# Order of the first loads and of one transpose step in a fused sliding-window attention and MLP kernel

## The chip, the cores and the metric

The kernel runs on one core of one Trainium2 chip. The metric is device time in microseconds: 308.39 us before the change, the median of three runs (308.27 to 308.43).

## The reference, cut to what matters

```python
# q, k, v: (8 batches, 8 heads, 576 positions, 64), f32
scores = scale * q @ k.T                    # scale = 1/8
mask = abs(pos[:, None] - pos[None, :]) <= 32
attn = softmax(where(mask, scores, -1e9))
x = (attn @ v).transpose(0, 2, 1, 3).reshape(4608, 512)
h = x @ w_in                                # (512, 2048)
g = where(h >= 1, h, where(h <= -1, 0, (h + 1) ** 2 / 4))
out = g @ w_out                             # (2048, 512), f32
```

## The kernel before

The inputs are f32 and everything is multiplied in bf16. All loads but two are issued by GpSimd, which casts them on the way. Two heads lie side by side in the 128 partitions, and the positions are cut into 9 chunks of 64; `vn` therefore has 18 chunks of v for one batch, chunks 0 to 8 for one pair of head groups (`y1 = 0`) and 9 to 17 for the other (`y1 = 1`).

```python
# S = 576, D = 64, NY = 4, NC = 9, DFF = 2048, NF = 8, TB = 256
def load_half(half, t, h, ...):      # half of q (t=0) or k (t=1) of batch 0, for 64 columns
    (eng or nc.gpsimd).dma_start(out=dst[0, half][:, h], in_=...)       # line 86

def load_rows(b, t):                 # q or k of batch 1, whole
    nc.gpsimd.dma_start(out=dst[b], in_=...)                            # line 93

def load_v(b, n):                    # a quarter of v of batch b: 64 partitions
    ...
    nc.gpsimd.dma_start(out=vn[b][64 * a:64 * a + 64, :, h], in_=...)   # line 107

def load_w_in(c0, c1, h):            # columns c0 to c1 of w_in, 64 partitions
    nc.gpsimd.dma_start(out=w_in[64 * h:64 * h + 64, :, c0:c1], in_=...)  # line 111

def load_w_out(c, k0, k1):           # 256 columns of w_out, rows of blocks k0 to k1
    nc.gpsimd.dma_start(out=w_out[:, k0:k1, 256 * c:256 * c + 256], in_=...)  # line 116
```

The loads at the start, in the order in which they are issued:

```python
for h in range(2):
    load_half(0, 0, h, (nc.sync, nc.scalar)[h], q32)    # q, first half: not GpSimd
for h in range(2):
    load_half(0, 1, h)                                  # k, first half
...
load_v(0, 0)
P.affine_select(out=step, ...)
for n in range(1, 4):
    load_v(0, n)
...
cuts = [0, 256, 512, 768, 1024, 1280, 1792, DFF]
w = [(load_w_in, c0, c1, h) for c0, c1 in zip(cuts, cuts[1:]) for h in range(2)]
put(w[:4] + [(load_half, 1, t, h) for t in range(2) for h in range(2)] + w[4:12])
put([(load_w_out, 0, 0, 4)] + w[12:])
put([(load_w_out, 0, k, k + 4) for k in range(4, 16, 4)] + [(load_rows, 1, t) for t in range(2)])
put([(load_v, 1, n) for n in range(4)])
```

The main loop goes through 144 positions, called slots here. In slot `a` the first product makes 256 columns of h for 256 tokens (`f = a % 8`, so slot `a` of the first eight reads w_in's columns 256a to 256a + 255), ScalarE and VectorE make g of it, and other work is hung behind the slot:

```python
def project(hp, f, r0, todo, first, last):              # hp has two buffers
    for n, (j, kk) in enumerate(todo):
        nc.tensor.matmul(hp[:, j], w_in[:, kk, 256 * f + 128 * j:...], xT[:, kk, r0:r0 + TB], ...)  # line 489

for a in range(...):
    post = [...]                     # output steps: pairs = [(6, 0), (7, 1), (8, 2), (9, 3), (11, 4), (12, 5), ...]
    ...
    project(...)                     # slots 0 and 1 together, then one by one
    A.activation(rr, hp, AF.Relu, scale=0.5, bias=0.5)  # line 533
    if a in (1, 7, 8, 9, 10, 11, 12):
        A.activation(mx, rr, AF.Square)                 # line 536
        V.scalar_tensor_tensor(g, hp, 1.0, mx, op0=ALU.max, op1=ALU.min)   # line 537
    else:
        V.tensor_max(mx, hp, rr)                        # line 539
        V.scalar_tensor_tensor(g, rr, 1.0, mx, op0=ALU.min, op1=ALU.mult)  # line 540
    run(a)                           # attention work that stands at this slot
    for x in post:
        pair(x)                      # the output step: 8 matmuls of g with four blocks of w_out, line 464
```

Before slot 0 the kernel makes the first 256 tokens of batch 0's attention: transposes of q's and k's first halves, scores, `sums(0, 0, 0, TB)` and `sums(0, 1, 0, TB)`, each of which multiplies with `vn` and with ones (line 295) and ends in ScalarE's ln and exp (lines 301, 302) and VectorE's product into xT (line 307). What stands at the slots that matter here:

```python
at(1, (tposes, 0, (0, 1), (1, 1)))                  # second halves of q and k of batch 0
at(2, (scores, 0, (0, 1), (0, 2), (2, 4)), (scores8, 0, ps_o))
at(3, (scores, 0, (1, 2), (0, 2), (2, 4), ps_n), (sums, 0, 0, TB, MAIN, ps_s))
at(4, (sums, 0, 1, TB, MAIN))                       # y1 = 1, tokens 256 to 479
at(5, (sums, 0, 0, MAIN, S, ps_s))                  # tokens 480 to 575
at(13, seq[0][1])                                   # first scores of batch 1
...
for t in range(2):
    at(11 + t, (tposes, 1, (t, 0), (t, 1)))         # q of batch 1 behind slot 11, k behind slot 12
```

`tposes` is 36 transposes on TensorE (line 189) and four copies out of PSUM (line 192), two on ScalarE and two on VectorE.

Of the kernel before, what the change touches and what calls it, by code (L numbers as in the profile page):

```python
# [14 lines left out]
def kernel(  # L15
# [19 lines left out]
    nc = tc.nc  # L35
    B, H, S, D = q.shape
    NT, DM, DFF = out.shape[0], 512, 2048
    NY = H // 2
    NC = S // 64
# [38 lines left out]
    qn, kn, vn = {}, {}, {}  # L78
# [20 lines left out]
            nc.gpsimd.dma_start(out=x[:, :, h], in_=src[b, NY * h:NY * h + NY].rearrange("y s d -> (y s) d")  # L99
                                .rearrange("(u p) d -> p u d", p=128))  # L100

    def load_v(b, n):
        if b not in vn:
            vn[b] = nat.tile([128, 2 * NC, 2, D], BF, name="vn", tag="vn", bufs=3)
        h, a = divmod(n, 2)
        y = NY * h + 2 * a
        nc.gpsimd.dma_start(out=vn[b][64 * a:64 * a + 64, :, h], in_=v[b, y:y + 2].rearrange("y s d -> (y s) d")  # L107
                            .rearrange("(c r) d -> r c d", r=64))

    def load_w_in(c0, c1, h):  # L110
        nc.gpsimd.dma_start(out=w_in[64 * h:64 * h + 64, :, c0:c1],  # L111
# [11 lines left out]
    for h in range(2):  # L123
# [5 lines left out]

    step = early.tile([128, 257], BF, name="step")  # L130
    V.memset(step, 0.0)
    load_v(0, 0)
    P.affine_select(out=step, in_=step, compare_op=ALU.is_ge, fill=-1.0, base=-65, channel_multiplier=-1,
                    pattern=[[1, 257]])
    for n in range(1, 4):
        load_v(0, n)
    V.memset(ones, 1.0)
    for t in qTs:
        V.memset(t[:, 0:PAD], 0.0)
# [4 lines left out]
    def put(todo):  # L144
        for fn, *x in todo:
            fn(*x)

    cuts = [0, 256, 512, 768, 1024, 1280, 1792, DFF]
    w = [(load_w_in, c0, c1, h) for c0, c1 in zip(cuts, cuts[1:]) for h in range(2)]
    put(w[:4] + [(load_half, 1, t, h) for t in range(2) for h in range(2)] + w[4:12])  # L150
    put([(load_w_out, 0, 0, 4)] + w[12:])
    put([(load_w_out, 0, k, k + 4) for k in range(4, 16, 4)] + [(load_rows, 1, t) for t in range(2)])
    put([(load_v, 1, n) for n in range(4)])
    P.tensor_copy(band[HD[1], 0:128], band[HD[1], 64:192])
    for m, n, x in ((mask4, 8, 128), (mask8, 4, TAIL)):
# [229 lines left out]
    def at(a, *todo):  # L385


        ev.setdefault(a, []).extend(x for x in todo if x)
# [24 lines left out]
    for n, a in enumerate(sl):  # L413
        at(a, seq[6 + n][0], seq[7 + n][1] if n < len(sl) - 1 else None)
    for t in range(2):
        at(11 + t, (tposes, 1, (t, 0), (t, 1)))
    loads, xps = {}, {16: [(2, 0)], 18: [(2, 1)]}
    for b in range(LONG + 1, B):
        a = sl[5 * (b - 1) - 7] - 17
# [75 lines left out]
    for a in range(NF * NB + 2 * NF):  # L495
# [11 lines left out]
        if a < NF * NB:  # L507
            if wide:
                n, f = divmod(a - WIDE[0], 2 * NF)
                t = WIDE[0] // NF + 2 * n  # L510
# [6 lines left out]
            else:  # L517
                t, f = divmod(a, NF)
# [30 lines left out]
        if a >= 40:  # L549
            n = (4, 3, 3)[a % 3] if a < 88 else 4  # L550
# [36 lines left out]
```

The softmax here doesn't subtract the row's maximum and nothing guards it: scores larger than these inputs give would overflow.

## Time and profile before

| what | value |
| --- | --- |
| time, median of three | 308.39 us |
| span of the profiled run | 306.1 us |
| granted TensorE clock | 1.00 |
| TensorE matmuls, share of the span | 97% |
| VectorE, ScalarE, GpSimd | 78%, 62%, 25% |
| start of the first slot | 13.24 us |
| idle time of TensorE before that slot and slots 1, 2 and 11 | 0.44, 0.67, 0.72, 0.33 us |

The page of a profile gives busy times and the chain of work that ended last. A timeline lists the instructions of an engine in order of time, with equal neighbours merged: start, length, engine, line, operation, the tiles that it writes and reads, the shape and a count; in brackets stand the idle time just before it and what ended it. PE is TensorE, PEld its weight loads, DVE is VectorE, ACT is ScalarE, POOL is GpSimd, SP is SyncE. A bar of GpSimd that issues a load is not the transfer; the landing of a load is told apart, as the time from the bar's start. The view by stretches gives each engine's busy time within a stretch, with the number of instructions, then the granted clock, the share of the DMA engines and GB/s, counted in the bytes that are written.

### The profile page before, as it was taken

How to read it: one execution, taken by the hardware profiler on the slowest of the kernel's cores; microseconds unless marked ns; L12 is line 12 of the kernel's file. 1: busy time of each engine (PE TensorE's matmuls, PEld its weight loads, DVE VectorE, ACT ScalarE, POOL GpSimd, SP SyncE). 2: the span in 40 equal slices, each digit the busy share in tenths (PEclk: the TensorE clock that was granted, in tenths of full speed). 3: DMA queues.
4: the chain of work that ended last, by engine and by line, in shares of the span. 5: the costliest groups of instructions: out<-in, count | busy, mean ns of one | idle time of the engine just before them, and what ended most of it. 6: DMA issues, size and time to landing. Idle time of an engine off the chain costs nothing.

```text
span 306.1 us, 7974 instructions
## 1 busy us (share of the span) xinstructions
PE 298.4 (97%) x3388; PEld 181.2 (59%) x3388; DVE 239.6 (78%) x376; ACT 191.2 (62%) x320; POOL 77.1 (25%) x92
## 2 busy tenths in 40 slices
PE   8889999999999999999999999999999999999995
PEld 3468878876666676666654544444445444446644
DVE  3268568888888989998999998888888888788700
ACT  3688896748856856776766766665667654444311
POOL 8787661037009009004600900000000000000000
PEclk9999999999999999999999999999999999999999
DMA  9999999999999999999998991550101000000121
GB/s 153 184 197 198 186 196 153 173 156 164 139 186 109 181 169 124 165 144 116 148 127 166 145 156 39 111 115 34 36 34 37 36 34 35 36 34 34 59 80 69
DMA packets 137171, 35.67 MB, mean 117 GB/s; under 512 B 122160, under 2 KB 132912, under 8 KB 137136
## 3 DMA queue, kind: packets, MB, share of 16 engines
q0 software_dynamic: 102976, 18.06, 83.5%
q1 hardware_dynamic: 34016, 16.81, 26.1%
q8 instruction: 26, 0.43, 0.6%
q10 hardware_dynamic: 144, 0.29, 0.3%
q14 instruction: 9, 0.07, 0.1%
HBM read 36.70 MB, written 9.44 MB: 151 GB/s over the span
## 4 chain that ended last, share of the span: by engine, by line
PE 91%; POOL 3%; DMA 2%; ACT 1%; issue 1%; DVE 0%; POOLq 0%; ACTq 0%
PE op L449 36%; PE hp L489 22%; PE hp L514 18%; PE bb L295 6%; PE op L464 4%; PE bb L229 2%; DMA w_in<-in_moe_w_in_dram 2%; POOL vn L107 1%; PE op L440 1%; POOL w_in L111 1%; PE tp L189 1%; ACT pt L237 1%; POOL kh L86 1%; POOL qh L86 0%; PE bb L208 0%
## 5 line engine op out<-in xcount | busy, mean ns | idle before, releaser
L533 ACT ACTIVATE rr<-hp 128x512 f32<-128x512 f32 x144 | 85.5, 595 | 86.1 <-PE hp L514 41.7
L449 PE MATMUL op<-w_out,gT 128*128 128x512 bf16 x496 | 126.9, 380 | 0.0
L539 DVE TENSOR_TENSOR mx<-hp,rr 128x512 f32<-128x512 f32 x137 | 94.4, 689 | 26.1 <-ACT rr L533 24.3
L540 DVE SCALAR_TENSOR_TENSOR gT<-rr,mx 128x512 bf16<-128x512 f32 x137 | 94.8, 692 | 4.7
L489 PE MATMUL hp<-xT,w_in 128*128 128x256 bf16 x640 | 83.1, 273 | 2.2 <-DMA w_in<-in_moe_w_in_dram 1.4
L489 PEld LDWEIGHTS <-w_in 128*128 128x128 bf16 x640 | 61.8, 98 | 22.7 <-issue 2.8
L449 PEld LDWEIGHTS <-gT 128*128 128x128 bf16 x496 | 46.1, 98 | 45.2
L514 PE MATMUL hp<-xT,w_in 128*128 128x512 bf16 x256 | 65.7, 379 | 0.0
L514 PEld LDWEIGHTS <-w_in 128*128 128x128 bf16 x256 | 25.0, 98 | 30.2
L99 POOL DMA_DIRECT2D qn<-in_q_dram x12 | 14.6, 1224 | 89.5 <-DMA kT<-kn 87.4
L237 ACT ACTIVATE pt<-bb 128x1024 bf16<-128x1024 f32 (+1 forms) x33 | 32.7, 1001 | 4.5 <-PE bb L229 3.1
L107 POOL DMA_DIRECT2D vn<-in_v_dram x32 | 27.7, 900 | 4.8 <-DMA w_out<-in_moe_w_out_dram 4.0
L307 DVE TENSOR_TENSOR xT<-bb,rc 128x512 bf16<-128x512 f32 (+1 forms) x32 | 21.0, 657 | 9.6 <-ACT rc L302 8.7
L453 ACT COPY osb<-op 128x512 f32<-128x512 f32 x31 | 18.0, 580 | 11.4 <-PE op L449 11.1
L302 ACT ACTIVATE rc<-lr 128x512 f32<-128x512 f32 (+2 forms) x40 | 23.5, 587 | 1.3
L301 ACT ACTIVATE lr<-bb 128x512 f32<-128x512 f32 (+2 forms) x40 | 22.1, 552 | 0.3 <-PE bb L295 0.3
L203 DVE TENSOR_TENSOR pt<-pt,mask 128x1024 bf16<-128x1024 bf16 (+1 forms) x33 | 20.3, 614 | 0.5 <-ACT pt L237 0.5
L295 PE MATMUL bb<-pt,ones 64*64 64x256 bf16 (+3 forms) x352 | 19.6, 255 | 0.1
L295 PE MATMUL bb<-pt,vn 64*64 64x128 bf16 (+3 forms) x712 | 18.4, 204 | 0.1
L295 PEld LDWEIGHTS <-ones 64*64 64x64 bf16 x352 | 10.3, 105 | 11.6 <-issue 11.6
L295 PEld LDWEIGHTS <-vn 64*64 64x64 bf16 x712 | 16.7, 107 | 0.3 <-DMA vn<-in_v_dram 0.3
L464 PE MATMUL op<-w_out,gT 128*128 128x256 bf16 x128 | 16.5, 273 | 0.0
(61 smaller groups left out, 140.3 us busy)
## 6 DMA issues: line engine op xcount, KB each, us to landing
out_dram<-osb SPq DMA_DIRECT2D x35, 256.0 KB, 2.3
vn<-in_v_dram POOLq DMA_DIRECT2D x32, 144.0 KB, 9.7
qn<-in_q_dram POOLq DMA_DIRECT2D x12, 288.0 KB, 6.2
kn<-in_k_dram POOLq DMA_DIRECT2D x12, 288.0 KB, 9.0
w_in<-in_moe_w_in_dram POOLq DMA_DIRECT2D x12, 128.0 KB, 5.6
w_out<-in_moe_w_out_dram POOLq DMA_DIRECT2D x4, 256.0 KB, 8.0
w_out<-in_moe_w_out_dram POOLq DMA_DIRECT2D x2, 512.0 KB, 13.2
kh<-in_k_dram POOLq DMA_DIRECT2D x4, 144.0 KB, 5.4
```

Source lines behind the costliest of these rows:

```text
L107: nc.gpsimd.dma_start(out=vn[b][64 * a:64 * a + 64, :, h], in_=v[b, y:y + 2].rearrange("y s d -> (y s) d") .rearrange("(c r) d -> r c d", ...
L237: A.activation(p, ps[:, :, :w * n].rearrange(like, y=m), AF.Exp, scale=D ** -0.5)
L295: nc.tensor.matmul(bb[HD[h], a, o + c0:o + c1], ones[HD[a]] if c is None else vn[b][HD[a], c, h], p(a, h), start=n == 0, stop=True, skip_g ...
L301: A.activation(lr[:, :, :D0], bb[:, :, D0:2 * D0], AF.Ln)
L302: A.activation(rc[:, :, :D0], lr[:, :, :D0], AF.Exp, scale=-1.0)
L449: nc.tensor.matmul(op[tt], gT[:, j, home(tt // 2), 128 * (tt % 2):128 * (tt % 2) + 128], w_out[:, j], start=j == 0, stop=j == 15)
L464: nc.tensor.matmul(o[:, tt], gT[:, j, p, 128 * tt:128 * tt + 128], w_out[:, j, 256 * half:256 * half + 256], start=not done, stop=len(done ...
L489: nc.tensor.matmul(hp[:, j], w_in[:, kk, 256 * f + 128 * j:256 * f + 128 * j + 128], xT[:, kk, r0:r0 + TB], start=first and n == 0, stop=l ...
L514: nc.tensor.matmul(hp.rearrange("p n t -> p (n t)"), w_in[:, kk, 128 * f:128 * f + 128], xT[:, kk, r0:r0 + 2 * TB], start=n == 0, stop=n == 3)
L533: A.activation(rr, hp, AF.Relu, scale=0.5, bias=0.5)
L539: V.tensor_max(mx, hp, rr)
L540: V.scalar_tensor_tensor(g, rr, 1.0, mx, op0=ALU.min, op1=ALU.mult)
```

## The change

Three things are changed, and no arithmetic.

1. The first v (batch 0) is loaded in two parts: chunks 0 to 13 where it stood, and chunks 14 to 17 later. The first part is all that the sums before slot 0 and those behind slot 3 read; chunks 14 to 17 are first read behind slot 4. The four loads of the second part are put one by one behind the four loads of w_in for slots 2 and 3.
2. w_in is loaded in pieces of 256 columns throughout. Before, the columns of slots 5 and 6 (1280 to 1791) came in one piece of 512, so that slot 5 waited for slot 6's columns too. The first load of w_out still stands in front of the last two pieces.
3. The transposes of q of batch 1 stand behind slot 10 instead of slot 11. Those of k stay behind slot 12.

The aim is to let slots 0 to 3 start with fewer bytes ahead of them in the queue, to let slot 5 start on its own columns, and to put work on TensorE between slots 10 and 11.

```diff
-    def load_v(b, n):
+    def load_v(b, n, c0=0, c1=2 * NC):
...
-        nc.gpsimd.dma_start(out=vn[b][64 * a:64 * a + 64, :, h], in_=v[b, y:y + 2].rearrange("y s d -> (y s) d")
-                            .rearrange("(c r) d -> r c d", r=64))
+        nc.gpsimd.dma_start(out=vn[b][64 * a:64 * a + 64, c0:c1, h], in_=v[b, y:y + 2].rearrange("y s d -> (y s) d")
+                            .rearrange("(c r) d -> r c d", r=64)[:, c0:c1])
...
-    load_v(0, 0)
+    load_v(0, 0, 0, 14)
...
     for n in range(1, 4):
-        load_v(0, n)
+        load_v(0, n, 0, 14)
...
-    cuts = [0, 256, 512, 768, 1024, 1280, 1792, DFF]
-    w = [(load_w_in, c0, c1, h) for c0, c1 in zip(cuts, cuts[1:]) for h in range(2)]
-    put(w[:4] + [(load_half, 1, t, h) for t in range(2) for h in range(2)] + w[4:12])
-    put([(load_w_out, 0, 0, 4)] + w[12:])
+    w = [(load_w_in, c, c + 256, h) for c in range(0, DFF, 256) for h in range(2)]
+    put(w[:4] + [(load_half, 1, t, h) for t in range(2) for h in range(2)]
+        + [x for n in range(4) for x in (w[4 + n], (load_v, 0, n, 14, 2 * NC))] + w[8:14])
+    put([(load_w_out, 0, 0, 4)] + w[14:])
...
     for t in range(2):
-        at(11 + t, (tposes, 1, (t, 0), (t, 1)))
+        at(10 + 2 * t, (tposes, 1, (t, 0), (t, 1)))
```

## The prediction

> **What bounds the kernel now.** I read the page's busy line first, then the chain that ended last, then the timelines of TensorE and GpSimd over the first 42 us, then the landing times of single loads.
>
> ```profile
> PE 298.4 (97%) x3388; PEld 181.2 (59%) x3388; DVE 239.6 (78%) x376; ACT 191.2 (62%) x320; POOL 77.1 (25%) x92
> ...
> PE 91%; POOL 3%; DMA 2%; ACT 1%; issue 1%; DVE 0%; POOLq 0%; ACTq 0%
> ```
>
> TensorE is the bound: 97% busy and 91% of the chain. What is not TensorE in the chain (POOL 3%, DMA 2%) lies at the start: printed in order of time, the chain is GpSimd issuing loads up to 12 us, then 6.31 us of a w_in load, and from 18.53 us TensorE nearly without a break. The change moves only what comes before slot 13, so I work with the timeline of that stretch. TensorE (start, length, what, and in brackets the idle time before it and what ended it):
>
> ```profile
> 13.24 0.60 PE L489 MATMUL hp<-xT,w_in 128*128 128x256 bf16 x4 [0.44 <-DVE xT L307]
> 14.50 1.47 PE L489 MATMUL hp<-xT,w_in 128*128 128x256 bf16 x12 [0.67 <-DMA w_in<-in_moe_w_in_dram]
> ...
> 17.12 0.69 PE L189 MATMUL tp<-ident,kh 128*64 128x128 bf16 x17 [0.47 <-DMA kh<-in_k_dram]
> 18.53 1.03 PE L489 MATMUL hp<-xT,w_in 128*128 128x256 bf16 x8 [0.72 <-DMA w_in<-in_moe_w_in_dram]
> ...
> 26.99 1.04 PE L489 MATMUL hp<-xT,w_in 128*128 128x256 bf16 x8
> 27.86 1.04 PE L464 MATMUL op<-w_out,gT 128*128 128x256 bf16 x8
> ...
> 32.23 1.04 PE L489 MATMUL hp<-xT,w_in 128*128 128x256 bf16 x8
> 33.59 1.03 PE L489 MATMUL hp<-xT,w_in 128*128 128x256 bf16 x8 [0.33 <-DVE gT L537]
> 34.55 1.20 PE L189 MATMUL tp<-ident,qn 128*64 128x128 bf16 x36
> 35.68 1.05 PE L464 MATMUL op<-w_out,gT 128*128 128x256 bf16 x8
> ```
>
> Slots 0 and 1 start at 13.24, slot 2 at 18.53, slot 7 at 26.99, slot 10 at 32.23, slot 11 at 33.59. The reader is to see five pauses: 0.44 for xT, then 0.67, 0.47 and 0.72 for loads, then 0.33 in front of slot 11 for VectorE's gT of slot 9 (hp has two buffers). GpSimd, which issues every load with a cast:
>
> ```profile
> 11.42 1.95 POOL L111 DMA_DIRECT2D w_in<-in_moe_w_in_dram  x3
> 14.65 1.83 POOL L111 DMA_DIRECT2D w_in<-in_moe_w_in_dram  x3 [1.28 <-DMA w_in<-in_moe_w_in_dram]
> 16.65 1.33 POOL L111 DMA_DIRECT2D w_in<-in_moe_w_in_dram  x2 [0.17 <-issue]
> ```
>
> Of these loads the one at 14.65 is the eighteenth. It starts 0.28 after the tenth landed (issued 8.38, 6.0 to landing, so 14.37). The twenty-first starts at 16.65, 0.28 after the thirteenth landed (16.36). So I read a rule into it: **a load waits until the load eight before it has landed.** Last, the DMA rate, from the view by stretches (busy time of the engines, then PEclk, DMA share, GB/s):
>
> ```profile
> 6.00:10.00 4.00, 3.81 (x85) 2.45 (x83) 1.35 (x2) 2.57 (x5) 3.99 (x7) 1.00 2.72 152
> 10.00:14.00 4.00, 3.29 (x67) 1.74 (x65) 0.91 (x2) 3.39 (x6) 3.07 (x6) 1.00 1.38 199
> 14.00:18.00 4.00, 2.84 (x48) 2.24 (x48) 2.24 (x4) 2.40 (x5) 3.05 (x5) 1.00 1.35 195
> ```
>
> The rate is flat at 195 to 199 while w_in is loaded, and 152 while v is loaded. The queue does not run dry: the loads are served in order, and each waits for the bytes ahead of it.
>
> **What the Trainium skill says.** "DMA: Bandwidth & Descriptors", section "Why small descriptors are slow (HBM only)", has a fixed cost on every descriptor, 27% for one of 256 bytes; v is read in rows of 64 f32, that is 256 bytes, and the trace agrees (152 against 195 GB/s). "Perfetto Trace Analysis", section "DMA Optimizations", says that splitting a load helps it start sooner if the DMA engines are otherwise idle; here they are not, so I expect the splits to change the order of arrival and not the total. The same page, section "DMA Instruction — SWDGE (GPSIMD)", says that the bar on GpSimd is descriptor generation and not the transfer; the trace agrees: a w_in bar is 0.61, its landing 4.6 to 6.4 after its start.
>
> **The change part by part.**
>
> *Part 1, the first v cut to 14 chunks.* Four loads lose 4 of 18 chunks: 4 x 64 partitions x 4 chunks x 128 bytes written = 131 kB. At 152 GB/s that is 0.86 us by which everything behind the v loads arrives earlier: w_in of slots 0 and 1, then q's and k's second halves. What this opens on TensorE: the v wait inside the first sums (0.31 on the weight loads) goes, so xT comes some 0.25 earlier, since ScalarE is busy with pt until 10.93 and its ln now starts at 11.20. The 0.67 pause goes (the load lands at about 13 instead of 14.37); k's half lands at 16.2 instead of 17.08; slot 2's w_in, with one v piece (0.2) ahead of its second half, lands at 17.7 instead of 18.40. Slot 2 should start at 17.6 to 17.9, a lead of 0.6 to 0.9.
>
> *Part 2, the v pieces and the split w_in.* The same 131 kB come back between w_in's pieces, so from slot 4's w_in on no bytes are saved. New are 6 loads: 4 v pieces and 2 halves of w_in. Each costs GpSimd about 0.6 (a w_in bar has 256 descriptors, as a v piece has), 3.6 in all; the shortened v bars give back little (an estimate: 0.89 for 1152 descriptors and 0.61 for 256 make 0.3 ns each, so 4 x 256 x 0.3 = 0.3 us). GpSimd waits 1.28 + 0.42 + 0.50 + 0.73 between loads today, so most of the 3.6 fits there, but with eight loads in flight and four of them only a third as long, fewer bytes are queued. An estimate with the bars, the landing spread and the eight-load rule put in order by hand: the queue runs dry for 1.0 to 1.5 us in total between the third v piece and slot 4's w_in. The slowest of the DMA engines should hide about 1.2 of that, because I take it to be behind the others today: the w_in load at 8.38 landed 1.9 after the one before it (14.37 against 7.78 + 4.7), where 0.67 is usual, and the delay stays. What remains, with two 512-column loads cut (2.6 between landings for both today, against 4 x 0.67), is +0.1 to +0.4 for everything behind slot 5's w_in. Slot 5's own w_in comes about 1.2 earlier (22.6 instead of 23.70), since it no longer waits for slot 6's half.
>
> *What becomes of the lead.* The second output step at 27.86 needs the second piece of w_out, issued at 20.08 and landing 7.7 later, at 27.80: **no slack today.** All the bytes ahead of it are the same after the change. So the lead of 0.6 to 0.9 at slot 2 ends there: the step starts at 27.9 to 28.2, that is 0 to 0.3 later than today. The early gain is swallowed.
>
> *Part 3, q's transposes in slot 10.* TensorE's work is only reordered: slot 11's 8 matmuls (0.98 in the chain) and 36 transposes (1.12) change places. Today the 0.33 pause plus start-up before slot 11 is lost: slot 10 ends at about 33.2, slot 11 starts at 33.59. After, the transposes need q of batch 1, issued at 22.74 and landing 10.6 later, 33.34; with +0.1 to +0.4 it lands at 33.45 to 33.75. They start there, end 1.12 later, slot 11 follows (0.98), and the next output step starts at 35.55 to 35.85, against 35.68 today.
>
> *Sum.* -0.13 to +0.17 at 35.7 us, from these steps alone. Behind it TensorE runs on; k's transposes at 37.53 need a load that lands at 36.18 (1.3 of slack), v of batch 1 lands at 41.16 for sums at 42.76 (1.6 of slack). The later stages have no changed instruction, so the shift is carried to the end.
>
> **Rivals.** *A: the lead survives.* If the DMA queue has slack that I do not see, because v pieces are served beside w_in at less cost, w_out and q land earlier, and up to 0.9 us of the lead at slot 2 plus the 0.33 pause would reach the end: 307.2 to 307.6. For it: the rate of 152 for v means that the DMA engines are not at their byte limit there. Against it: the flat 195 to 199 after. *B: GpSimd becomes the bound.* If the eight-load rule starves the queue by more than the slowest engine's lag, w_out and q land 0.6 to 1.0 later, and slot 10's transposes stall TensorE where slot 11 used to run: 308.8 to 309.3. For it: 6 more loads and a wait of 1.28 that exists already. Against it: 2.9 us of waits between loads that can absorb them. *C: nothing is moved*, because the q load decides either way: 308.2 to 308.4. This is nearest to my sum.
>
> **Range and chances.** I lean a little to the fast side of the sum, as A costs nothing to be partly true and the 0.33 pause is sure to go: 308.1, with 307.4 (most of A) to 308.8 (mild B) for 8 in 10. A move of 2% would be 6.2 us; all pauses of this stretch together are 0.44 + 0.67 + 0.47 + 0.72 + 0.33 = 2.6 us, so neither side of 2% can be reached this way.
>
> **What would show it.** Slot 2's first matmul at 17.6 to 17.9 shows part 1 right. A pause in front of the second output step at about 28, ended by w_out, shows the lead swallowed; no pause and a start under 27.5 shows rival A. The transposes of q behind slot 10 with a wait of 0.1 to 0.5 for the q load, and no gT wait before slot 11, show part 3. GpSimd pauses before the third and fourth v piece and before slot 4's w_in, with a DMA rate under 190 GB/s from 17 to 20 us, show the starved queue. The prediction is wrong if q of batch 1 lands before 33.0 or after 34.0, or if a stage after 50 us changes its waits by more than a few tenths.

## The result and the profile after

The changed kernel takes 310.66 us (median of six runs, 310.31 to 311.26), against 308.35 us (308.11 to 308.57) for six runs of the kernel before on the same chip: a ratio of 1.0075, with a 95% interval of 1.0062 to 1.0088. It is slower by 2.3 us, and outside the range. The profiled span is 308.5 us against 306.1.

From the page of the kernel after, the line of busy times and the shares of the chain that ended last:

```profile
PE 293.6 (95%) x3350; PEld 181.4 (59%) x3388; DVE 240.0 (78%) x376; ACT 191.6 (62%) x320; POOL 80.4 (26%) x98
...
PE 85%; DMA 7%; POOL 4%; issue 2%; ACT 1%; POOLq 0%; ACTq 0%
```

The chain has changed: DMA holds 7% of it instead of 2%. Its longest pieces in order of time (start, length, what) name the loads:

```profile
8.49 5.62 DMA qh<-in_q_dram
16.90 2.41 POOL w_in L111 x4
19.32 5.94 DMA w_in<-in_moe_w_in_dram
25.54 10.49 DMA qn<-in_q_dram
36.07 1.20 PE tp L189 x36
```

Up to 36 us the end is now set by a wait of GpSimd for q's half, by GpSimd's issuing, and by the loads of w_in and of q of batch 1. TensorE's timeline shows the same from its side:

```profile
13.13 1.03 PE L489 MATMUL hp<-xT,w_in 128*128 128x256 bf16 x8
...
17.62 1.05 PE L489 MATMUL hp<-xT,w_in 128*128 128x256 bf16 x8 [0.92 <-DMA w_in<-in_moe_w_in_dram]
...
22.42 1.03 PE L489 MATMUL hp<-xT,w_in 128*128 128x256 bf16 x8 [0.89 <-DMA w_in<-in_moe_w_in_dram]
...
26.07 1.03 PE L489 MATMUL hp<-xT,w_in 128*128 128x256 bf16 x8 [0.69 <-DMA w_in<-in_moe_w_in_dram]
27.35 1.03 PE L464 MATMUL op<-w_out,gT 128*128 128x256 bf16 x8 [0.25 <-DMA w_out<-in_moe_w_out_dram]
28.79 1.03 PE L489 MATMUL hp<-xT,w_in 128*128 128x256 bf16 x8 [0.41 <-DMA w_in<-in_moe_w_in_dram]
30.55 1.03 PE L464 MATMUL op<-w_out,gT 128*128 128x256 bf16 x8 [0.73 <-DMA w_out<-in_moe_w_out_dram]
...
36.07 1.20 PE L189 MATMUL tp<-ident,qn 128*64 128x128 bf16 x36
37.19 1.05 PE L489 MATMUL hp<-xT,w_in 128*128 128x256 bf16 x8
```

Slot 2 starts at 17.62, earlier by 0.91. Slot 4 waits 0.89 and starts at 22.42, later than the 22.18 of before; slot 6 waits 0.69 and slot 7 waits 0.41. The second output step starts at 30.55 instead of 27.86, the transposes of q at 36.07. The loss arises between 20 and 31 us. The view by stretches says where, first before, then after (busy times with counts, clock, DMA share, GB/s):

```profile
17.00:20.00 3.00, 2.16 (x49) 1.65 (x53) 2.45 (x4) 2.00 (x4) 2.76 (x5) 1.00 1.41 196
20.00:23.00 3.00, 3.00 (x88) 2.37 (x76) 2.18 (x4) 3.00 (x7) 2.58 (x5) 1.00 1.29 199
23.00:26.00 3.00, 2.92 (x74) 2.26 (x72) 2.42 (x4) 2.94 (x7) 1.77 (x3) 1.00 1.44 192
```

```profile
17.00:20.00 3.00, 2.38 (x45) 1.71 (x46) 2.60 (x5) 2.22 (x4) 3.00 (x6) 1.00 1.33 126
20.00:23.00 3.00, 2.11 (x60) 1.61 (x58) 2.11 (x4) 2.97 (x7) 2.60 (x5) 1.00 1.16 143
23.00:26.00 3.00, 2.38 (x69) 1.70 (x66) 2.47 (x5) 2.84 (x6) 2.66 (x4) 1.00 1.29 160
```

The last number is the one to read: for nine microseconds the DMA engines move 126, 143 and 160 GB/s instead of about 195. What is missing is (195 - 126) x 3 + (195 - 143) x 3 + (195 - 160) x 3 = 468 kB, which is 2.4 us at 195 GB/s: as much as the whole loss. From 26 us on the rate is 196 again. GpSimd's timeline over the same time:

```profile
12.96 0.61 POOL L107 DMA_DIRECT2D vn<-in_v_dram  x1 [0.15 <-issue]
14.40 0.61 POOL L111 DMA_DIRECT2D w_in<-in_moe_w_in_dram  x1 [0.83 <-DMA qh<-in_q_dram]
...
16.90 3.67 POOL L111 DMA_DIRECT2D w_in<-in_moe_w_in_dram  x6
```

It waits once, 0.83 for the load eight before, and then issues without a break from 14.40 to 21.9. The bars at 16.25 and 16.90 begin 0.28 after the load eight before them has landed, so the eight-load rule holds GpSimd back there too, without a visible pause. GpSimd is behind the DMA engines and cannot get ahead of them.

### The profile page after: what moved, and what is told of

Its sections match the earlier page's. It is cut to its first block, busy times and chain, and to the rows that moved or that the text cites. A ratio compares the mean times of both kernels' runs of the same rounds, so it can differ in the third digit from the quotient of the medians.

```text
span 308.5 us, 7943 instructions
## 1 busy us (share of the span) xinstructions
PE 293.6 (95%) x3350; PEld 181.4 (59%) x3388; DVE 240.0 (78%) x376; ACT 191.6 (62%) x320; POOL 80.4 (26%) x98
## 4 chain that ended last, share of the span: by engine, by line
PE 85%; DMA 7%; POOL 4%; issue 2%; ACT 1%; POOLq 0%; ACTq 0%
PE op L449 34%; PE hp L489 20%; PE hp L514 18%; PE bb L295 6%; PE op L464 4%; DMA qn<-in_q_dram 3%; PE bb L229 2%; POOL w_in L111 2%; DMA w_in<-in_moe_w_in_dram 2%; DMA qh<-in_q_dram 2%; POOL vn L107 1%; PE op L440 1%; PE tp L189 1%; ACT pt L237 1%; POOL kh L86 0%
## 5 line engine op out<-in xcount | busy, mean ns | idle before, releaser
L449 PE MATMUL op<-w_out,gT 128*128 128x512 bf16 x460 | 119.5, 379 | 5.0 <-issue 4.8
L107 POOL DMA_DIRECT2D vn<-in_v_dram x36 | 29.7, 851 | 5.0 <-DMA w_out<-in_moe_w_out_dram 4.2
```

The costliest lines, as they stand in the source:

```text
L107: nc.gpsimd.dma_start(out=vn[b][64 * a:64 * a + 64, c0:c1, h], in_=v[b, y:y + 2].rearrange("y s d -> (y s) d") .rearrange("(c r) d -> r c ...
L449: nc.tensor.matmul(op[tt], gT[:, j, home(tt // 2), 128 * (tt % 2):128 * (tt % 2) + 128], w_out[:, j], start=j == 0, stop=j == 15)
```

## What the experiments ask

Four readings were to be told apart: the move of the transposes costs the time; the smaller loads slow the DMA engines by their size or by the partitions that they write; GpSimd's extra issue time does it; or the queue runs short because small loads take places among the eight in flight. All runs are in one table. The time is the median and the ratio that to the kernel before on the same chip, with its interval. **Time to turn** was worked out from the trace load by load: from the start of a load's issue to the first landing of the load before it (a load lands in 16 parts), when its own turn comes; the column has the shortest from 13 us on. Rates and times to turn are each of one profiled run.

| run | us | ratio (95%) | GB/s in 17-20, 20-23, 23-26 us | shortest time to turn, us |
| --- | --- | --- | --- | --- |
| before | 308.4 | 1 | 196, 199, 192 | 2.65 |
| after | 310.66 | 1.0075 (1.0062 to 1.0088) | 126, 143, 160 | 1.79 |
| slot10 | 307.92 | 0.9983 (0.9976 to 0.9990) | 192, 199, 194 | 2.48 |
| w256 | 308.16 | 0.9995 (0.9984 to 1.0006) | 191, 190, 186 | 2.41 |
| slot10w256 | 307.89 | 0.9988 (0.9981 to 0.9994) | 190, 188, 193 | 2.34 |
| vsplit | 311.70 | 1.0107 (1.0057 to 1.0157) | 128, 133, 172 | 1.57 |
| fourmore | 312.46 | 1.0126 (1.0068 to 1.0184) | 129, 126, 170 | 1.50 |
| fourshort | 312.97 | 1.0149 (1.0113 to 1.0185) | 105, 143, 166 | 1.26 |
| fourbusy | 309.47 | 1.0054 (1.0032 to 1.0076) | 178, 140, 167 | 1.60 |
| grouped | 310.16 | 1.0056 (1.0041 to 1.0072) | 134, 120, 146 | 1.24 |
| wide23 | 309.75 | 1.0048 (1.0033 to 1.0063) | 169, 147, 148 | 1.76 |
| twoshort | 311.65 | 1.0132 (1.0093 to 1.0171) | 156, 118, 169 | 1.67 |
| fourlate | 308.36 | 1.0002 (0.9994 to 1.0011) | 195, 204, 191 | 2.43 |
| wide01 | 311.14 | 1.0091 (1.0069 to 1.0114) | 129, 121, 136 | 1.36 |
| twoshortwide01 | 310.02 | 1.0055 (1.0038 to 1.0072) | 157, 132, 181 | 1.96 |
| slot10wide01 | 307.96 | 0.9990 (0.9978 to 1.0003) | 191, 187, 190 | 2.19 |
| wideall | 310.57 | 1.0070 (1.0044 to 1.0095) | 196, 194, 202 | 2.71 |
| twoshortwideall | 309.72 | 1.0055 (1.0037 to 1.0072) | 204, 200, 199 | 3.18 |

In eight of these kernels some runs have a lower granted clock over the span, 0.987 to 0.994: one of five in fourbusy, two of four in vsplit, fourmore, twoshort and twoshortwideall, three of four in fourshort and wide23, four of six in wideall. Their medians hold that as well. At 0.998 or more, vsplit takes 310.50 and 310.69 us, fourmore 310.56 and 311.23, fourshort 311.32, twoshort 310.45 and 311.08: 2.1 to 3.0 us more than the kernel before, about what the change costs.

## The three parts alone

**slot10** is the kernel before with part 3 alone:

```diff
-        at(11 + t, (tposes, 1, (t, 0), (t, 1)))
+        at(10 + 2 * t, (tposes, 1, (t, 0), (t, 1)))
```

> Part 3 alone: q of batch 1 transposed behind slot 10, all loads as before. Theory S (the DMA queue is starved by the added loads): none is added here, so q lands at 33.3 as before, its transposes start at 33.4, and the kernel gains 0.1 to 0.3 us. Theory H (loads of 64 partitions keep half of the DMA engines busy, and two in a row for the same half leave the other half idle): the same, 0.1 to 0.3 us faster. Theory Q (it is the transposes' new place that costs): slower by 1 us or more.

It is faster by 0.17%, or 0.5 us. In the profiled run slot 5 waited 0.72 for its load, so TensorE was 0.49 behind the kernel before at slot 7 (27.48 against 26.99); its timeline there and around the move:

```profile
24.34 1.03 PE L489 MATMUL hp<-xT,w_in 128*128 128x256 bf16 x8 [0.72 <-DMA w_in<-in_moe_w_in_dram]
...
27.48 1.04 PE L489 MATMUL hp<-xT,w_in 128*128 128x256 bf16 x8
...
33.68 1.20 PE L189 MATMUL tp<-ident,qn 128*64 128x128 bf16 x36
34.81 1.05 PE L489 MATMUL hp<-xT,w_in 128*128 128x256 bf16 x8
35.69 1.04 PE L464 MATMUL op<-w_out,gT 128*128 128x256 bf16 x8
```

No wait stands before slot 11, and the output step starts at 35.69 against 35.68 before: the move gave the 0.49 back. The transposes are not the cause, and this part works.

**w256** has part 2's cuts alone (16 loads of w_in instead of 14), **slot10w256** adds part 3:

```diff
-    cuts = [0, 256, 512, 768, 1024, 1280, 1792, DFF]
+    cuts = list(range(0, DFF + 1, 256))
```

> Part 2 alone: w_in in 256-column pieces, two loads more, in alternating halves of the partitions, no v moved. Theory S: two loads more cost GpSimd 1.2 us of issue, of which part is hidden by its waits: 0.1 to 0.6 us slower. Theory H: halves still alternate, so no change beyond 0.2 us either way.

> Parts 2 and 3 without the v split: w_in in 256-column pieces and q transposed in slot 10. From the two runs alone (0.5 us faster, 0.3 faster to nothing): 307.7 to 308.0, so 0.3 to 0.7 us faster than before, if the effects add. It is the candidate for a version that beats both.

w256 is as fast as before, slot10w256 as slot10. Two loads more are free where they stand.

**vsplit** has part 1 alone, with the old cuts of w_in:

```diff
...
-    put(w[:4] + [(load_half, 1, t, h) for t in range(2) for h in range(2)] + w[4:12])
+    put(w[:4] + [(load_half, 1, t, h) for t in range(2) for h in range(2)]
+        + [x for n in range(4) for x in (w[4 + n], (load_v, 0, n, 14, 2 * NC))] + w[8:12])
```

> Part 1 alone: v's last four chunks in four loads of their own between w_in's pieces; w_in's later pieces stay at 512 columns, transposes stay. Theory S: four loads more, 2.4 us of issue: the queue runs dry from 17 us on, 1 to 2 us slower. Theory H: the order is lower, lower, upper, upper half: 1.5 to 2.5 us slower. Theory Q: no slower than before.

It loses 1.07%, and its two runs at a clock of 0.998 and 1.00 take as long as the three parts together. The loss is that of the split v.

## What it is in the split

**fourmore** leaves v whole and adds four loads that nothing reads, of 256 descriptors of 16 bytes, at the places of the v pieces; **fourshort** makes them 64 descriptors each, so that neither their bytes nor their packets count; **fourbusy** puts a GpSimd copy of 0.62 us in each of these places, and no load:

```diff
-    put(w[:4] + ... + w[4:12])
+    put(w[:4] + ...
+        + [x for n in range(4) for x in (w[4 + n], (load_none, n))] + w[8:12])
...
+    def load_none(n):                        # in fourmore
+        nc.gpsimd.dma_start(out=none[...], in_=v[0, ..., 0:256]...[:, :, 0:8])
+    def load_none(n):                        # in fourshort
+        nc.gpsimd.dma_start(out=none[...], in_=v[0, ..., 0:64, 0:32])
+    def busy(n):                             # in fourbusy, in the place of load_none
+        P.tensor_copy(none, warm)
```

> The kernel before with four small loads put between w_in's pieces, where the change has the v pieces: 256 descriptors each, 16 bytes each into a scratch that nothing reads (an addition: nothing is left out). They carry next to no bytes. Theory S: the same 2.4 us of issue and the same places among the eight loads in flight as the v pieces, so a DMA rate well under 195 GB/s from 17 us on and 0.8 to 2 us slower. Theory H: w_in's halves still alternate and the small loads are over at once, so under 0.4 us slower.

> The kernel before with four loads of only 64 descriptors (128 bytes each, into a scratch) where the earlier run had four loads of 256 descriptors. Issue time goes down little (some 0.5 us each), the packets for the DMA engines go down to a quarter. Theory F (places in flight) and theory I (issue time): nearly the same loss as with 256 descriptors, 1.5 us or more. Theory P (it is the many short packets that the DMA engines have to serve): at most 0.5 us slower.

> The kernel before with GpSimd kept busy: four copies of 128 x 512 bf16 into a scratch (some 0.6 us each) where the change has its four v pieces, and no load added. Theory I (issue time: GpSimd's 2.4 us of extra work alone starve the DMA queue): a DMA rate of 110 to 140 GB/s at 17 to 23 us and 1.5 to 3 us slower, like the four small loads. Theory F (places in flight: what costs is that small loads take half of the eight places, so that half as many bytes are queued, which copies do not do): at most 0.6 us slower.

Both kinds of load cost about as much as the split v, so neither their bytes nor the number of their packets is the cause. fourbusy, without any load, still takes the rate down, as its view by stretches shows:

```profile
17.00:20.00 3.00, 1.97 (x38) 1.39 (x32) 2.97 (x5) 2.18 (x4) 3.00 (x6) 1.00 1.36 178
20.00:23.00 3.00, 3.00 (x93) 2.39 (x93) 1.83 (x4) 2.95 (x6) 3.00 (x5) 1.00 1.06 140
23.00:26.00 3.00, 1.84 (x41) 1.43 (x39) 2.39 (x5) 2.94 (x6) 1.36 (x3) 1.00 1.24 167
```

POOL is busy for 3.00 of 3.00 us in the first two stretches and the rate falls to 140 in the second: no small load is needed, and the cost of 1.1 us lies between the two expectations. This is not GpSimd's time alone, as the slowest DMA engine also lags more here: the sixteen parts of the tenth load land within 2.67 us, against 2.02 in the kernel before.

**grouped** is the kernel after with the four v pieces behind all four w_in loads of slots 2 and 3 instead of between them. It asked whether the alternation of the two 64-partition halves matters:

```diff
-        + [x for n in range(4) for x in (w[4 + n], (load_v, 0, n, 14, 2 * NC))] + w[8:14])
+        + w[4:8] + [(load_v, 0, n, 14, 2 * NC) for n in range(4)] + w[8:14])
```

> The changed kernel with the four v pieces behind all four w_in loads of slots 2 and 3, not between them. Number of loads, bytes and issue time are as in the changed kernel; only the order differs, and halves of the partitions alternate. Theory H (halves): the loss goes, 308.3 or less. Theories I, F and P: within 0.8 us of the changed kernel, since the same loads pass through the same queue; slots 2 and 3 start a little earlier, slot 4 no earlier.

The rate stays at 120 to 146. With fourmore, where w_in's halves alternate and the time is lost all the same, this rules the alternation out.

**wide23** is the kernel after with 512 columns per load of w_in for slots 2 and 3, and for 5 and 6, and with the v pieces behind slots 2 and 3; **twoshort** adds only two of the 64-descriptor loads to the kernel before; **fourlate** puts the four loads of fourshort behind slot 7's w_in, among the w_out loads, issued from 20.0 to 26.0 us, 3.0 to 4.7 us ahead of their turn:

```diff
+    cuts = [0, 256, 512, 1024, 1280, 1792, DFF]                                   # wide23
...
+        + w[4:6] + [(load_v, 0, n, 14, 2 * NC) for n in range(4)] + w[6:10])
...
+        + [x for n in range(4) for x in (w[4 + n], (load_none, n))[:2 - n % 2]] + w[8:12])   # twoshort
...
-    put([(load_w_out, 0, k, k + 4) for k in range(4, 16, 4)] + ...
+    put([x for n, k in enumerate(range(4, 16, 4)) for x in ((load_none, n), (load_w_out, 0, k, k + 4))]
+        + [(load_none, 3)] + ...                                                  # fourlate
```

> The changed kernel with fewer loads: w_in of slots 2 and 3 in one 512-column piece per half, the four v pieces behind it, slots 5 and 6 in one 512-column piece again as before. Together with v's split that is four loads fewer than the changed kernel and as many as the kernel before (30 up to the q of batch 1 before, 34 after, 30 here, within one), the same bytes. If the number of loads up front is the cause: the DMA rate from 17 to 23 us back to 180 or more and 307.6 to 308.6. If it is the v split itself (its bytes or its order): 310 or more, as in the changed kernel. Slot 2 starts later than in the changed kernel, near 18.3, since it waits for slot 3's columns too.

> The kernel before with two small loads of 64 descriptors in place of four (behind the first and the third w_in load of slots 2 and 3). If the loss is a threshold (GpSimd's lead over the DMA engines is used up), two loads cost much less than half of what four cost (3.0 to 4.6 us): under 1 us. If each load costs the same: 1.5 to 2.3 us.

> The kernel before with the same four small loads put later, around the three later w_out loads, where a load lands some 8 us after its issue in the kernel before, so the queue is long. If what costs is that the queue is short where the loads are put: at most 0.6 us slower. If each load costs wherever it stands: 3 us slower as before.

The first two fail my expectation: wide23 still loses 0.48% where after loses 0.75% (it has 31 loads up to q of batch 1, not quite as few as the 29 of before), and two small loads cost nearly as much as four, so the cost is no sum of issue times. fourlate is free: it is not the loads, it is where they stand.

## Too few bytes in flight

If a load must be issued some time before its turn, the table's last column should sort the runs, and of those told of so far it does: the five that keep their rate have 2.34 or more, those that lose it 1.79 or less. The first try at giving the time back put w_in's first 512 columns in one load per half, so two loads fewer stood in front (`cuts = [0, 512, 768, ...]`), in the kernel after (**wide01**), in twoshort (**twoshortwide01**) and in slot10 (**slot10wide01**). For wide01:

```diff
-    w = [(load_w_in, c, c + 256, h) for c in range(0, DFF, 256) for h in range(2)]
-    put(w[:4] + ...
+    cuts = [0] + list(range(512, DFF + 1, 256))
+    w = [(load_w_in, c0, c1, h) for c0, c1 in zip(cuts, cuts[1:]) for h in range(2)]
+    put(w[:2] + ...
```

> The kernel after with w_in's first 512 columns (slots 0 and 1, which are computed together) in one load per half, so two loads fewer stand in front of the split v pieces. Theory, GpSimd's lead: in the kernels that lost time the first load of the stretch from 16.5 to 18 us landed 2.4 to 2.9 us after its issue began, in those that lost none 3.1 us or more; two loads fewer of 256 descriptors should give GpSimd about 0.5 us more of lead. Then the lead stays over 3.1 us, the DMA rate from 17 to 23 us is 180 GB/s or more, and the time is 307.4 to 308.4 us. Rival, the split v pieces themselves (four small loads among w_in's) slow the queue whatever the lead: rate 125 to 150 GB/s from 17 to 23 us and 310 us or more.

> The kernel before with the two added loads of 64 descriptors that cost 3 us, and w_in's first 512 columns in one load per half, so that the number of loads is that of before. Lead theory: the two loads removed in front pay for the two added; first landings stay 3 us or more behind their issue, rate 180 GB/s or more from 17 to 26 us, time 308.2 to 308.9 us. Rival, the short loads themselves disturb the DMA queue whatever GpSimd's lead: rate 115 to 160 GB/s and 310.5 us or more, as in the run with the two loads alone.

> The kernel before with q's transposes behind slot 10, and w_in's first 512 columns in one load per half; v whole. Two loads fewer than before. Lead theory: the queue is as full as before (190 to 199 GB/s from 17 to 26 us), and the time is that of the slot move alone, 307.7 to 308.1 us. Rival: larger first pieces make slot 0 wait longer than 13.24 us, by 0.1 to 0.3 us, which is swallowed at the second output step, so the time is the same 307.8 to 308.2 us. Either way below the kernel before by 0.1 to 0.2%.

wide01 failed: no gain, time to turn 1.36. Taking loads out in front does not help, because GpSimd's lead there is not set by its issuing but by the wait for the load eight before (0.95, 0.75 and 0.93 us at the loads issued at 11.99, 13.35 and 14.90). twoshortwide01 went half of the way (1.96), and slot10wide01, at 2.19, holds 187 to 191.

What sets the time to turn can be worked out. A load held back by the rule is issued 0.28 after the eighth before it has landed on the slowest DMA engine (in the 18 traces no load whose landings are recorded is issued sooner); until its turn the seven between must be moved:

time to turn = bytes of seven loads / 195 GB/s - lag of the slowest engine - 0.28.

In the kernel before, the load issued at 14.65 has four halves of q and k (147 kB) and three w_in loads (131 kB) ahead: 983 kB, 5.04 - 2.02 - 0.28 = 2.74, measured 2.65. In the kernel after, the load issued at 14.40 has three halves, two w_in loads and two v pieces (33 kB): 769 kB, 3.94 - 1.74 - 0.28 = 1.92, measured 1.96. The lag is the time from the first to the last landing of the eighth load before. A v piece takes a place among eight and holds a quarter of the bytes of a w_in load. The formula holds while the rate does: for the load issued at 16.90 in the kernel after, which has its shortest time, it gives (4 x 33 + 3 x 131) / 195 - 1.39 - 0.28 = 1.02, and 1.79 was measured, since the loads ahead were by then late themselves.

So the deciding pair keeps every small load and doubles the bytes of the others: all of w_in in 512-column loads, in the kernel after (**wideall**) and in twoshort (**twoshortwideall**).

```diff
-    w = [(load_w_in, c, c + 256, h) for c in range(0, DFF, 256) for h in range(2)]
+    w = [(load_w_in, c, c + 512, h) for c in range(0, DFF, 512) for h in range(2)]
...
-    put(w[:4] + [(load_half, 1, t, h) for t in range(2) for h in range(2)]
-        + [x for n in range(4) for x in (w[4 + n], (load_v, 0, n, 14, 2 * NC))] + w[8:14])
-    put([(load_w_out, 0, 0, 4)] + w[14:])
+    put(w[:2] + [(load_half, 1, t, h) for t in range(2) for h in range(2)]
+        + [x for n in range(4) for x in (w[2 + n], (load_v, 0, n, 14, 2 * NC))])
+    put([(load_w_out, 0, 0, 4)] + w[6:])
```

> The kernel after with all of w_in in 512-column loads (262 kB each, one per half), the four second parts of v still put one by one behind loads three to six. In the ten kernels that lost time the shortest time from the start of a load's issue to its turn (first landing of the load before it) was 1.24 to 1.96 us, in the six that lost none 2.19 us or more. Theory, the bytes held by the loads in flight decide: with four loads of 33 kB among seven the other three now hold 262 kB each, 917 kB / 195 GB/s less about 2 us of lag, so 2.6 us or more, and GpSimd issues at about 400 GB/s, so the DMA rate stays 180 GB/s or more from 17 to 26 us and the time is 307.6 to 308.7 us, although slot 2 now waits for slot 3's columns (about 18.9 us). Rival, small loads among w_in's disturb the queue whatever is in flight: 125 to 155 GB/s from 17 to 26 us and 309.7 us or more.

> The kernel before with the two added loads of 64 descriptors that cost 3 us, and all of w_in in 512-column loads. Theory of the bytes in flight: the shortest time from issue to turn is 2.6 us or more, rate 180 GB/s or more from 17 to 26 us, time within 0.6 us of the kernel before (308.2 to 308.9 us; slot 2 waits about 0.6 us longer for its larger load, and the second output step needs its w_out as late as before). Rival, the small loads as such: 115 to 165 GB/s and 310 us or more.

wideall, by stretches, and then its slot 2 on TensorE:

```profile
17.00:20.00 3.00, 0.80 (x16) 0.61 (x11) 2.04 (x4) 1.20 (x2) 2.17 (x4) 1.00 1.40 196
20.00:23.00 3.00, 3.00 (x89) 2.22 (x91) 1.38 (x2) 2.44 (x6) 2.55 (x5) 1.00 1.43 194
23.00:26.00 3.00, 2.92 (x81) 2.27 (x77) 2.29 (x4) 2.95 (x6) 2.42 (x4) 1.00 1.28 202
```

```profile
19.49 1.03 PE L489 MATMUL hp<-xT,w_in 128*128 128x256 bf16 x8 [2.21 <-DMA w_in<-in_moe_w_in_dram]
```

The rate holds at 194 to 202 with the split v in place, and at 199 to 204 with the two short loads: on the rate, the reading by the bytes in flight came true and that of the small loads as such did not. The formula gives (4 x 33 + 3 x 262) / 195 - 1.75 - 0.28 = 2.67 for the shortest, measured 2.71. On the time I was wrong for both. Slot 2 must now wait for slot 3's columns, 2.21 us, and starts at 19.49 where I had 18.9; slot 6 waits 0.59 more, and the output step behind slot 11 starts 1.1 later than before (36.81 against 35.68). The profiled wideall has 309.03 us; the other five runs have 309.56 to 311.72, four of them with a granted clock of 0.987 to 0.994 over the span, so part of their excess is clock and not loads. twoshortwideall waits 1.90 before slot 0 and 2.03 before slot 2. Large loads cure the queue and delay their readers. The pair also halves the number of w_in's loads and doubles their packets to 1,024 bytes; wide23 and twoshort have such packets in part and lose, but no run separates these from the bytes in flight. Nor did any run let more than eight loads be in flight.

In fourbusy the bytes in flight are those of before, and at its shortest time to turn the load is issued 1.15 after the eighth before it has landed: there GpSimd is late by its copies, for which the formula has no term.

**What stays open** is how a short time to turn becomes so long a loss. It tells whether the rate falls, not how much is lost: grouped has the shortest (1.24) and loses 1.8 us, fourshort has 1.26 and loses 4.6. Nor is it the load with the short time that must come late: in twoshort three loads issued 2.01, 1.79 and 1.67 ahead of their turn land 0.57 to 0.69 after the one before, as they should, and the next one lands 2.42 after. In the kernel after, GpSimd issues 131 kB every 0.60 us from 16.9 us on, 217 GB/s, and by 21.3 us a load is 4.6 from its turn, yet the rate needs until 26 us to recover. In these 9 us 56 packets of 512 bytes took over 150 ns each, 20 us of engine time together, where 60 ns is usual and the kernel before has three. Such packets go with the loss: those of 512 or 1,024 bytes and over 200 ns number 25 to 52 in the ten runs that lose their rate and 0 to 10 in the eight that keep it. Spread over 16 DMA engines they are 0.7 to 1.7 us, a good part of what is missing; what holds them up, and whether the short queue does, was not found.

## Why the prediction was wrong, by its steps

- **TensorE as the bound, and only the stretch before slot 13:** right. ScalarE's first operation of each slot is 2.38 to 2.39 us later from slot 12 to the end, a constant shift. No later stage changed.
- **Part 1:** right but for two sizes. xT comes 0.11 earlier and not 0.25. Slots 0 and 1 start at 13.13 without the v wait and the 0.67 pause, slot 2 at 17.62 (17.6 to 17.9 predicted), a lead of 0.91. Slot 3 still has 0.71 of it (19.52 against 20.23). That slot 5's w_in would come 1.2 earlier was wrong: it lands at 23.73 against 23.70.
- **Part 2 is the step that failed.** Its sentence was that the queue runs dry for 1.0 to 1.5 us in total, of which the slowest engine hides 1.2, so that +0.1 to +0.4 remain. Two terms of it were wrong. The first shortfall was sized well: up to slot 4's w_in, which has the same bytes ahead of it, 1.18 us are lost (its last part lands at 22.29 instead of 21.11). But in the end the slowest engine hides none of that. Its lag shrinks only as far as slot 3's load, whose parts land within 0.91 us; at slot 4's two loads the spread is 2.30 and 1.69 again. It also works the other way: the eight-load rule waits for exactly that engine, so its lag is taken off the time to turn, 1.74 us at the load issued at 14.40. And I let the queue be full again at once. From 17 to 20 us 207 kB are missing, 1.06 us, and from 20 to 26 us another 261 kB, 1.34 us. The sum is 2.4 instead of 0.1 to 0.4.
- **The lead is swallowed at the second output step:** wrong in place and size. The lead is gone at slot 4 (22.42 against 22.18). The step had no slack, as said, and passes the loss on: w_out lands at 30.51, and the step starts at 30.55 after a pause of 0.73, not at 27.9 to 28.2.
- **Part 3:** right in kind. Slot 11 follows q's transposes without a wait, and the run with this part alone gains 0.5 us. Its date was wrong with part 2: q lands at 36.02, not at 33.45 to 33.75, 2.68 later than before; less the pause of 0.33 that is gone, 2.35 are left, which is the shift to the end.
- **The rivals:** B named the mechanism, GpSimd as the bound by the eight-load rule, at 308.8 to 309.3. It was right in direction and under half of the size (0.4 to 0.9 us more, against 2.3), and my argument against it, that 2.9 us of GpSimd's waits could absorb the new issues, was the wrong one: only the first of them, 1.28, lies ahead of the loads in question and the others come after 22 us, and being free to issue is no use while eight loads are out.
- **The range** followed from that argument, and leant to the fast side for the 0.33 pause and for a rival A of which nothing came true.
- **The signs:** the rate under 190 GB/s from 17 to 20 us came (126), and q landed after 34.0. The pauses of GpSimd before the third and fourth v piece and before slot 4's w_in did not come: these bars begin at most 0.03 after the one before, and the one pause, 0.83, stands before slot 3's w_in. A queue can starve without them.
- **Two readings were loose.** A w_in load of the kernel before lands 4.6 to 7.0 us after its bar starts, not 4.6 to 6.4. And in the Trainium skill's "Perfetto Trace Analysis", section "DMA Optimizations", generally idle DMA engines are the condition for the whole task to end sooner; without it splitting may still let some parts start sooner. That the splits would change the order and not the total was wrong here: the rate fell from 196 to 126 GB/s.

The Trainium skill's page "DMA: Bandwidth & Descriptors", section "Anatomy of one DMA — SWDGE (gpsimd) path", gives a load issued by GpSimd a fixed cost of about 2.0 us beside its bytes. I had not used it. The traces agree in size: among all runs here no load's first landing came earlier than 1.85 us after its issue began, and the rate fell in every run whose shortest time to turn was 1.96 or less and in none with 2.19 or more. The page puts most of the 2.0 us at the end of a transfer; no run here divides it.

## A version that beats both

slot10, the kernel before with only the transposes moved, has the lowest ratio: 307.92 us, 0.9983 of before (0.9976 to 0.9990) where after has 1.0075. Finer cuts of w_in (slot10w256, 0.9988) or coarser ones in front (slot10wide01, 0.9990) add nothing that shows, as the three intervals overlap.

## What to carry to other kernels

Before a load is split in a queue with a fixed number of loads in flight, add up the bytes of the loads that would be in flight ahead of each new one: divided by the transfer rate, and less the lag of the slowest DMA engine, they must cover the time that a load needs from issue to its turn (here about 2 us). Where they do not, a small load costs far more than its bytes, and free time on the issuing engine elsewhere does not pay for it; put small loads where large ones are queued. A larger load repairs the queue but delays whoever reads its first part, so measure both.

## What was not expected of the hardware

- Two added loads of 64 descriptors, 8 kB written in all, cost 3.3 us (twoshort, 311.65 against 308.39; 2.1 and 2.7 in the two runs at a clock of 0.999 and 1.00) when issued at 12.4 and 15.1 us, and four cost nothing when issued from 20 us on (fourlate).
- In the kernel before, the last of the 16 parts of the w_in load issued at 8.38 lands at 14.37, 0.97 after the fifteenth, and one part of every later load of this stretch is late by as much; the spread of a load goes from 0.7-0.9 to 1.7-2.0 us. An instruction fetch of 16 kB starts at 12.06 in the trace and takes 0.98 us, which fits; leaving it out was not tried. By the formula this one lag takes about 1 us off the time to turn of every load.
- TensorE's granted clock can fall for a stretch after pauses: the Trainium skill's "Perfetto Trace Analysis", section "Matmul Optimizations", says that the engine scales power with its use, and fourshort shows it, where pauses of 1.15 and 1.43 us come just before 26.45 us. Its view by stretches, and that slot on TensorE:

```profile
26.00:29.00 3.00, 2.56 (x37) 1.72 (x38) 1.13 (x3) 0.88 (x2) 1.85 (x3) 0.58 1.40 182
```

```profile
26.45 1.86 PE L495 MATMUL hp<-xT,w_in 128*128 128x256 bf16 x8 [1.43 <-DMA w_in<-in_moe_w_in_dram]
```

The clock is 0.58, and eight matmuls that take 1.03 us elsewhere take 1.86. The trace has 3.41 us at half clock here, and wide23's has as much behind a pause of 2.43. An estimate from this: 3.41 x 0.5 / 310 takes the clock of a span to 0.994, and two such stretches to 0.989, the values of most of the runs named under the table. The length of a pause alone does not decide it: wideall's 2.21 and twoshort's 2.29 were followed by none. In after, with pauses of 0.7 to 0.9 us, the clock of the span is 0.998, so this is no part of its loss worth naming.
